# A planned adaLN block on one core: the order of its instructions and loads is made anew

## The chip, the cores and the metric

The kernel runs on one core of a Trainium2 chip. The metric is the device time of one execution in microseconds. Below, PE is TensorE, ACT ScalarE, DVE VectorE, POOL GpSimd and SP SyncE, which here only issues DMAs.

## What is computed

One transformer block with adaptive layer norm, for one sequence of S = 2048 rows and D = 640 columns, all in bfloat16:

```python
mod = (_silu(c) @ w_mod).reshape(c.shape[0], 6, 1, -1)
sa, ca, ga, sb, cb, gb = (mod[:, i] for i in range(6))
h = _layernorm(x) * (1 + ca) + sa
x = x + ga * _A_ref(h, A_wqkv, A_wo)          # 32 heads of 20, causal window of 256
h = _layernorm(x) * (1 + cb) + sb
x = x + gb * _B_ref(h, B_w_gate, B_w_up, B_w_down)   # (sigmoid(h wg) * (h wu)) wd, 1536 wide
```

(The loop over i stands for six assignments.) `w_mod` has 640 rows and 3840 columns; wqkv 640 x 1920, wo 640 x 640, the gate and up weights 640 x 1536, the down weight 1536 x 640.

## The kernel before, in words

**Chunks and blocks.** The sequence is cut into 8 chunks `a` of 256 rows, each of two blocks `b` of 128 rows. Per chunk there are these steps: load the two x blocks (tags x0 to x15, `load_x` with pool `x0`, four buffers); layer-norm statistics and normalization (`ln_stats`: `bn_stats` on L721, `bn_aggr` on L723, the power on POOL, L728, the normalization on L731); a transpose into `hT`, for chunks 0 and 1 by PE (`pe_transposes`), later by DMA (`transp_dma`), with scale and shift (`modulate`, L745 and L746); q, k and v projections (`qkv`, evacuated by `evac` on L792 of ACT or L793 of DVE), transposes of q and k; attention in score sets (four heads each, `score_set`: matmuls on L871, one exponential over 128 x 2048 on L882 of ACT, masks on POOL, L890 and L892), then `burst` with the product with v and its normalization (`norm`, L933 to L942), written to DRAM and read back transposed as `oT`; the output projection plus residual (`outproj`, L987), for which x is loaded a second time (tags y0 to y15, pool `x1`, six buffers); a second layer norm; the gated product (`mlp`, L1025, L1027), the down projection and the second residual add (L1042); the store.

Nearly all matmuls show one line of the helper `mm`, L636 (whole tiles) or L637 (tiles of heads), and all plain DMAs show L524.

**Weights and modulation.** All weights are loaded once and stay. The three thirds of `w_mod` are loaded first into memory that later holds other things: third 0 (`wm0`) into `wd`, third 1 (`wm1`) into `wu`, third 2 (`wm2`) into `hh`. Their products with silu(c) give the shifts and scales for the two layer norms, and `gbc`, by which DVE multiplies `wo` (L1066) and `wd` (L1011). Third 0 is needed before the first `hT` (copy `mA`, L707); `shB` (L1060) is a short DVE copy of another product.

**The order.** Nothing runs in the order in which the program names it. Each step is recorded by `Prog.op` with a list of engines, a planned duration, its dependencies, a priority (`prio` plus an entry of the table `PRI` by tag) and an earliest time `tmin`. `Prog.schedule` then places one step after the other: for each engine it takes, of the steps whose planned start lies within a small width of the earliest (0.04 us, for PE `PE_EPS`), that of the lowest priority number; of the engines it takes the one that starts first. Buffers are handed out in the same pass. For DMAs the plan has one variable `bw`, the time up to which the 16 DMA engines are taken. `emit` writes the order of each engine out as a fixed program with semaphore waits. The plan's times are used for nothing else: on the chip each engine goes through its list, and an instruction waits for its semaphores with all that stands behind it on its engine.

**Queues.** All DMAs go to SP but three: `c_row` and the x blocks 0 and 1, which ACT issues. The large loads (wv, wm1, wo, wm2, wg, wu, wd) are a chain: each waits for the one three places ahead of it (`chain`, DEEP = 3). Score sets have an earliest planned time `PACE0 + PACE * n`.

**Before, at the start,** SP issues x2, five parts of wm0, two of wq, two of wk, x3, wv and on; ACT issues x0, c_row, x1. PE runs matmuls on zeros until the first products with `w_mod` are there.

Of the kernel before, what the change touches and what calls it, by code (L numbers as in the profile page):

```python
# [8 lines left out]
ALU = mybir.AluOpType  # L9
# [5 lines left out]
H = 32  # L15
DH = 20
# [64 lines left out]
class Prog:  # L81
# [67 lines left out]
    def schedule(self):  # L149
        free = {e: 0.0 for e in ENGS}  # L150
        bw = 0.0
# [68 lines left out]
        while placed < n:  # L220
            best = None
            for e in ENGS:
# [5 lines left out]
                for o in c.values():  # L228
                    st = max(free[e] + (SWITCH if e == "pe" and o.mode != pemode else 0.0), o.ready)
                    if e == "dve" and o.port:  # L230
                        st = max(st, free["pool"])
                    elif e == "pool":
                        st = max(st, portend)
                    if o.tiles:
                        got = slots_for(o)
                        if got is None:
                            continue
                        st = max(st, got[0])
                    lst.append((st, o))
                    if tmin is None or st < tmin:  # L240
                        tmin = st
# [26 lines left out]
            if o.isdma:  # L268
                s0 = max(st + dur + 1.1, bw)
                bw = s0 + o.work  # L270
                o.end = bw + 0.7
# [118 lines left out]
def c_pe(n):  # L390
# [3 lines left out]
PE_EPS = 0.131  # L394
PRI = {
    "amodu2": 50.6, "amodu3": 100.7, "amodu4": 71.5, "amodu5": -83.8, "amodu6": 14.5, "amodu7": 25.1, "apow0": 50.2,
    "apow1": -22.7, "apow2": -37.9, "apow3": 26.2, "apow4": 37.9, "apow5": 2.4, "apow6": -29.7, "apow7": 20.3,
    "astats0": 2.8, "astats1": 0.5, "astats2": 0.4, "astats3": 134.9, "astats4": 103.8, "astats5": 149.6,
    "astats6": 33.7, "astats7": -18.8, "atr2": -1.5, "atr3": 36.3, "atr4": 0.4, "atr5": 6.4, "atr6": -17.8,
    "atr7": 32.3, "axh0": -4.4, "axh1": 29, "axh2": -1.6, "axh3": -4, "axh4": 6.9, "axh5": 15.3, "axh6": 0.6,  # L400
    "bmodu0": 11.1, "bmodu1": 54, "bmodu2": -3, "bmodu3": -7.5, "bmodu4": -47.5, "bmodu5": -2.3, "bmodu6": 5.7,
    "bmodu7": 60.8, "bpow0": -33.2, "bpow1": 14.6, "bpow2": 1.5, "bpow3": 1, "bpow4": 39.4, "bpow5": 82.1,
    "bpow6": -42.5, "bpow7": -21.3, "bstats0": 108.1, "bstats1": 8.1, "bstats3": 41.3, "bstats4": 61.6,
    "bstats5": 2.3, "bstats6": -14.7, "bstats7": -15.8, "btr0": 17.3, "btr1": 57.4, "btr2": 19.5, "btr3": 8.1,
    "btr4": 10.3, "btr5": 35.7, "btr6": -1.2, "btr7": -3.5, "bxh0": -14.2, "bxh1": -11.3, "bxh2": 18.2, "bxh3": -5.2,
    "bxh4": 2, "bxh5": 10.7, "bxh6": 59.4, "ctr": -8.6, "divide_0": -2.5, "divide_1": -38.1, "divide_2": -302.1,
    "divide_3": -25.2, "divide_4": 0.3, "divide_5": 32.3, "divide_6": -19.5, "divide_7": 20.5, "down0": 188.3,
    "down1": -19.9, "down2": -6.2, "down3": 118.6, "down4": 39.9, "down5": 1.1, "down6": 189.9, "down7": 296.8,
    "evqk0": -26.7, "evqk1": 40.4, "evqk2": 55.5, "evqk3": 11.1, "evqk4": 136.1, "evqk5": 44.7, "evqk6": -9.9,
    "evqk7": -0.3, "evqt0": -5, "evqt1": 5.6, "evv0": -5.5, "evv1": -10.9, "evv2": -29.4, "evv3": 1.8, "evv4": -1.8,  # L410
    "evv5": -0.4, "evv6": -4.1, "evv7": -12.7, "exp0": -20.6, "exp1": -20, "exp2": 18.1, "exp3": -0.8, "exp4": 35,
    "exp5": 41.7, "exp6": -96.1, "exp7": 17, "fill": -28.3, "glu_0": -19, "glu_1": 32.2, "glu_2": -32.7,
    "glu_3": 3.6, "glu_4": 6.6, "glu_6": -34.6, "glu_7": 63.5, "hTe0": 26.9, "hTe1": -6.9, "mask0": 27.5,
    "mask1": 25.2, "mask2": -21, "mask3": -12.1, "mask4": 63.1, "mask5": 16.4, "mask6": -2.3, "mask7": -22.1,
    "mlpg0": -25, "mlpg1": -24.5, "mlpg2": -24, "mlpu0": -25, "mlpu1": -24.5, "mlpu2": -24, "modA": -31.1,
    "modb": 2.1, "modc": -5.5, "n_ow_1": -73.7, "n_ow_2": -67, "n_ow_3": -11.5, "n_ow_4": 36.5, "n_ow_5": -4.9,
    "n_ow_6": 29.3, "n_ow_7": -1.9, "oT_0": 1.4, "oT_1": 16.1, "oT_2": 4.4, "oT_3": 37.2, "oT_4": 2.4, "oT_6": -15.9,
    "oT_7": -3.4, "out": -15.4, "projk0": -19.5, "projk2": 143.9, "projk3": -25.9, "projk4": 13.2, "projk5": 135.4,
    "projk6": -9.3, "projk7": -118.9, "projq0": -0.3, "projq3": -6, "projq4": 40.3, "projq5": 52.7, "projq6": -169.6,
    "projq7": -38.9, "projv2": 2.9, "projv3": 4.3, "projv4": 41.9, "projv5": 112.6, "projv7": 9.5, "ptr0": 6.6,  # L420
    "ptr1": 1.9, "pv1": -153.5, "pv2": -0.8, "pv3": -128.5, "pv4": 17.1, "pv5": -199.3, "pv6": 1.1, "pv7": 4,
    "qkt2": -0.1, "qkt3": 23.5, "qkt4": 210.5, "qkt6": -3.3, "qkt7": 39.1, "qtr0": -33.3, "qtr1": 1.7,
    "recip_0": -12.7, "recip_1": 25.7, "recip_2": -20.5, "recip_3": 18.8, "recip_4": 9.7, "recip_5": 75.9,
    "recip_7": 12.6, "res1_0": -27.2, "res1_1": -8.7, "res1_2": -8.7, "res1_3": 25.5, "res1_4": -28.5,
    "res1_5": -9.5, "res1_6": 10.7, "res1_7": 67.4, "res2_0": -5.2, "res2_1": -14.6, "res2_2": -0.5, "res2_3": 22,
    "res2_4": -19.6, "res2_5": -24.6, "res2_6": 93.7, "res2_7": 8.4, "score0": -27.9, "score1": -134.6,
    "score2": -18.3, "score3": -59.5, "score4": -289.6, "score5": 2.5, "score6": -20, "score7": -7.8, "tanh_0": 24.5,
    "tanh_1": 2.1, "tanh_2": -28.6, "tanh_3": -25.9, "tanh_4": -6.8, "tanh_5": 6.3, "tanh_6": 11.9, "tanh_7": 38.4,
    "tr1_1": 6.2, "tr1_2": -10.2, "tr1_3": -0.8, "tr1_5": -13.6, "tr1_6": 21.6, "tr1_7": 3.7, "tr2_0": -27.5,
    "tr2_1": 3.6, "tr2_2": 17.6, "tr2_3": 66.8, "tr2_4": 32, "tr2_5": -3.1, "tr2_6": 0.9, "tr2_7": -9.7, "wd": 3.7,  # L430
    "wds": -3, "wg": 8.7, "wk": -26.3, "wm0": -103, "wm1": 71.9, "wm2": -53.2, "wo": -48, "wo0": -23.5, "wo1": 4.4,
    "wo2": 13, "wo3": 15.4, "wo4": 24.1, "wo5": 28.9, "wo6": 29.6, "wo7": 14.8, "wos": 119.8, "wq": -27.7,
    "wu": 43.3, "wv": 3.2, "x0": -72.7, "x1": 14.7, "x10": 86.9, "x11": 65.2, "x12": 113.8, "x13": 107.7,
    "x14": 140.6, "x15": 301.2, "x2": -111.6, "x3": -19.2, "x4": 5, "x5": 8.7, "x6": 45.4, "x7": 45.5, "x8": 52.8,
    "x9": 60.4, "y0": -5.3, "y1": 45.5, "y10": 144.4, "y11": 91, "y12": 118.4, "y13": 163.1, "y14": 327.3,
    "y15": 235.6, "y2": 29, "y3": 73.8, "y4": 85.7, "y5": 17.2, "y6": 87.2, "y7": 163, "y9": 116.1,
# [6 lines left out]
PACE0 = -16.86  # L443
PACE = -0.757
# [4 lines left out]
WSE = ['dve', 'dve']  # L449


def build(nc, A_x, A_wqkv, A_wo, B_x, B_w_gate, B_w_up, B_w_down, c, w_mod, out, S=2048):
# [66 lines left out]
    def dma(dst, src, work, reads=(), writes=(), prio=50.0, tmin=0.0, tag="dma", extra=(), nonc=False, hold=(), eng="sp"):  # L519
# [5 lines left out]
        return A(eng, fn, 0.45, reads=reads, writes=writes, prio=prio, work=work, tmin=tmin, tag=tag, extra=extra, hold=hold)  # L525

    bulk = []

    def chain():
        return [bulk[-DEEP]] if len(bulk) >= DEEP else []  # L530
# [23 lines left out]
    def load_x(pool, b, prio, tmin=0.0, eng="sp"):  # L554
        t = Tile(pool, f"{pool.name}_{b}")
        dma(lambda: t.ap[:], lambda: x_flat[b * 128:(b + 1) * 128, :], 0.47 if b > 1 else 0.9, writes=[t.r()], prio=prio, tmin=tmin, tag=f"x{b}" if pool is p_x0 else f"y{b}",
            eng=eng)
# [9 lines left out]
    def load_wm(i, kt, prio, tmin=0.0):  # L567
        if i:
            bulk.append(dma(lambda: wm_ap[i][:, kt, :], lambda: wm_src[:, kt, i * 1280:(i + 1) * 1280], 0.86,
                            writes=[Rm[i][kt]], prio=prio, tag=f"wm{i}", extra=chain()))  # L570
            return bulk[-1]
        return dma(lambda: wm_ap[i][:, kt, :], lambda: wm_src[:, kt, i * 1280:(i + 1) * 1280], 1.12 - 0.06 * kt, writes=[Rm[i][kt]],
                   prio=prio, tmin=tmin, tag=f"wm{i}")

# [3 lines left out]
    def load_w3(k, prio, halves):  # L578
# [4 lines left out]
        if k == "wv":  # L583
            bulk.append(o)

# [8 lines left out]
    for kt in range(NDT):  # L594
        load_wm(1, kt, 0.4 + 0.01 * kt)
    bulk.append(dma(lambda: wo[:], lambda: A_wo.rearrange("(t p) f -> p t f", p=128), 2.2, writes=[R_wo], prio=0.5, tag="wo",
                    extra=chain()))
    for kt in range(NDT):
        load_wm(2, kt, 0.6 + 0.01 * kt)
# [109 lines left out]
    for kt in range(NDT):  # L709
        bulk.append(dma(lambda kt=kt: wg[:, kt, :], lambda kt=kt: B_w_gate.rearrange("(t p) f -> p t f", p=128)[:, kt, :], 1.03,  # L710
                        writes=[R_wg[kt]], prio=0.7 + 0.01 * kt, tag="wg", extra=chain()))

    def ln_stats(src, dst, prio, ln, a):
# [3 lines left out]
        def v(lo, w):  # L717
            return st.ap[:, lo:lo + w]
# [11 lines left out]
        for bi in range(n):  # L730
            A("dve", lambda e, g, bi=bi: e.tensor_scalar(dst[bi].ap[:], src[bi].ap[:], v(24 + 2 * bi, 1), v(30 + bi, 1),  # L731
                                                         op0=ALU.subtract, op1=ALU.mult), 0.44, port=True,
# [392 lines left out]
```

## Time and profile before

| what | value |
|---|---|
| median of 6 runs | 338.58 us (337.53 to 343.88) |
| the profiled execution, its own time | 338.71 us |
| its span, first to last instruction | 337.0 us |
| mean granted TensorE clock | 1.000 |
| DMA | 38.72 MB, mean 115 GB/s |
| first projection with wq | starts at 12.83 us |
| last matmul ends, last add starts | 334.7 us |

In the lines of the profile each engine has a busy time, its share of the span, and the number of instructions; PEld are the weight loads of TensorE. A row of forty digits cuts the span into equal slices of 8.4 us; a digit is the busy share in tenths. A line of windows has the stretch, its length, then busy time and number of instructions of PE, PEld, DVE, ACT and POOL, the granted clock, the DMA share and GB/s. A line of waits says which engine and line waited, for whom, then microseconds in total, how often, and the longest. A line of the timeline has start, length, engine, source line, operation, output and inputs; in brackets stands the idle time of the engine before it and what ended it.

### The profile page before, as it was taken

The page shows a single profiled execution, that of the slowest core. Times are in us where ns is not written, and L with a number is a line of the kernel's source. Part 1 is how long each engine was busy: PE and PEld are TensorE (multiplying, and loading weights), DVE is VectorE, ACT ScalarE, POOL GpSimd, SP SyncE. Part 2 cuts the span into 40 slices and gives each one's busy share as a digit, 9 for nine tenths or more (in the row PEclk, how much of TensorE's full clock was granted, in tenths as well). Part 3 has the DMA queues.
Part 4 walks back from the last instruction along what each step waited for, and adds up shares of the span by engine and source line. Part 5 has one row for each costly group of instructions (what it writes and reads, how often), then busy time and mean ns, then how long its engine had stood idle before and what let it go on. Part 6 is the DMA issues. An engine that isn't in the chain of part 4 may idle for free.

```text
span 337.0 us, 10072 instructions
## 1 busy us (share of the span) xinstructions
PE 326.2 (97%) x4146; PEld 232.2 (69%) x4146; DVE 227.4 (67%) x469; ACT 226.8 (67%) x215; POOL 160.8 (48%) x232
## 2 busy tenths in 40 slices
PE   8798989999899999999999999999999999999997
PEld 3555645657676667676666766776677787887875
DVE  5497988999889958553868567765558673553232
ACT  1386888897888989787889777897699440121200
POOL 4135466565587755575656674866576500010000
DMA  7987999979942981641383024220234041221001
GB/s 250 377 258 248 263 348 174 198 158 187 228 128 53 132 152 23 77 90 60 94 125 87 4 58 120 60 42 21 73 106 60 18 67 36 62 41 39 2 19 58
DMA packets 71686, 38.72 MB, mean 115 GB/s; under 512 B 46682, under 2 KB 68442, under 8 KB 71642
## 3 DMA queue, kind: packets, MB, share of 16 engines
q1 hardware_dynamic: 71344, 37.76, 48.4%
q8 instruction: 32, 0.52, 0.7%
q10 hardware_dynamic: 298, 0.33, 0.3%
q14 instruction: 12, 0.10, 0.1%
HBM read 21.96 MB, written 5.24 MB: 81 GB/s over the span
## 4 chain that ended last, share of the span: by engine, by line
PE 80%; DMA 10%; DVE 5%; issue 2%; ACT 1%; POOL 1%; SPq 0%; ACTq 0%; DVEq 0%
PE M L636 67%; PE S L637 7%; PE M L637 6%; DMA x<-in_A_x_dram 3%; DMA hT<-x 3%; DMA hh<-in_w_mod_dram 3%; DVE st L721 1%; DVE x L731 1%; DVE h2T L746 1%; DVE stg L793 1%; ACT E L882 1%; POOL st L728 0%; DVE T L933 0%; DVE hT L746 0%; SPq L524 0%
## 5 line engine op out<-in xcount | busy, mean ns | idle before, releaser
L882 ACT ACTIVATE E<-S 128x2048 bf16<-128x2048 f32 x90 | 168.9, 1877 | 30.3 <-PE S L637 28.8
L890 POOL TENSOR_SCALAR_AFFINE_SELECT E<-E 128x512 bf16<-128x512 bf16 (+2 forms) x90 | 77.2, 857 | 88.4 <-ACT E L882 88.1
L892 POOL TENSOR_SCALAR_AFFINE_SELECT E<-E 128x512 bf16<-128x512 bf16 (+1 forms) x84 | 69.4, 826 | 0.0
L636 PE MATMUL M<-h2T,wg 128*128 128x256 bf16 x480 | 63.1, 273 | 0.2 <-DVE h2T L746 0.2
L636 PE MATMUL M<-h2T,wu 128*128 128x256 bf16 x480 | 62.7, 273 | 0.0
L1025 ACT ACTIVATE sig<-M 128x512 f32<-128x512 f32 x48 | 28.6, 595 | 44.8 <-PE M L636 44.7
L1027 DVE SCALAR_TENSOR_TENSOR hh<-sig,M 128x512 bf16<-128x512 f32 x48 | 32.5, 677 | 35.4 <-PE M L636 26.5
L636 PE MATMUL M<-wd,hh 128*128 128x320 bf16 (+2 forms) x396 | 55.4, 295 | 0.0
L636 PEld LDWEIGHTS M<-h2T,wg 128*128 128x128 bf16 x480 | 44.9, 98 | 9.9 <-issue 2.5
L636 PEld LDWEIGHTS M<-h2T,wu 128*128 128x128 bf16 x480 | 45.7, 98 | 7.8 <-issue 2.1
L636 PEld LDWEIGHTS M<-wd,hh 128*128 128x128 bf16 x396 | 37.3, 98 | 14.8 <-issue 1.3
L637 PE MATMUL S<-QT,KT 20*128 20x256 bf16 (+1 forms) x960 | 35.9, 245 | 0.9 <-ACT E L882 0.9
L1042 DVE TENSOR_TENSOR x<-M,x 128x320 bf16<-128x320 f32 (+2 forms) x33 | 15.9, 481 | 26.5 <-PE M L636 26.3
L721 DVE BATCH_NORM_STATS2 st<-x 128x6 f32<-128x320 bf16 x64 | 28.9, 477 | 5.9 <-DMA x<-in_A_x_dram 5.8
L637 PEld LDWEIGHTS S<-QT,KT 20*128 20x128 bf16 x960 | 14.1, 92 | 21.0 <-ACT E L882 17.5
L933 DVE STREAM_TRANSPOSE T<-M 128x512 f32<-128x512 f32 x32 | 21.1, 694 | 10.8 <-PE M L637 10.7
L636 PE MATMUL M<-wq,hT 128*128 128x320 bf16 x160 | 25.3, 300 | 1.8 <-DVE stg L793 1.7
L726 POOL TENSOR_SCALAR st<-st 128x2 f32<-128x2 f32 x16 | 3.8, 235 | 46.2 <-DVE st L723 46.2
L636 PE MATMUL M<-wk,hT 128*128 128x320 bf16 x160 | 25.3, 300 | 0.2 <-DVE hT L746 0.2
L636 PE MATMUL M<-wv,hT 128*128 128x320 bf16 x160 | 25.1, 300 | 0.2 <-issue 0.2
L636 PE MATMUL M<-wo,oT 128*128 128x320 bf16 x160 | 24.6, 300 | 0.0
L637 PE MATMUL M<-E,V 128*32 128x256 bf16 (+1 forms) x960 | 22.7, 246 | 1.3 <-DVE shB L1060 1.2
(73 smaller groups left out, 318.5 us busy)
## 6 DMA issues: line engine op xcount, KB each, us to landing
x<-in_A_x_dram SPq DMA_DIRECT2D x30, 160.0 KB
doc<-On SPq DMA_DIRECT2D x64, 40.0 KB
out_dram<-x SPq DMA_DIRECT2D x15, 160.0 KB
wg<-in_B_w_gate_dram SPq DMA_DIRECT2D x5, 384.0 KB
wu<-in_B_w_up_dram SPq DMA_DIRECT2D x5, 384.0 KB
wd<-in_B_w_down_dram SPq DMA_DIRECT2D x4, 480.0 KB
wd<-in_w_mod_dram SPq DMA_DIRECT2D x5, 320.0 KB
wu<-in_w_mod_dram SPq DMA_DIRECT2D x5, 320.0 KB
```

The lines of the kernel that those rows point to most:

```text
L636: return e.matmul(o, l, r, start=st, stop=sp, skip_group_check=True)
L637: return e.matmul(o, l, r, start=st, stop=sp, tile_position=tp, skip_group_check=True)
L721: A("dve", lambda e, g, bi=bi, j=j: e.bn_stats(v(bi * 12 + j * 6, 6), src[bi].ap[:, j * 320:(j + 1) * 320]), 0.48, reads=[src[bi].r()], wr ...
L726: A("pool", lambda e, g: e.tensor_scalar(v(28, n), var(), EPS, None, op0=ALU.add), 0.2, reads=[st.r(("m", bi)) for bi in range(n)], writes ...
L731: A("dve", lambda e, g, bi=bi: e.tensor_scalar(dst[bi].ap[:], src[bi].ap[:], v(24 + 2 * bi, 1), v(30 + bi, 1), op0=ALU.subtract, op1=ALU.m ...
L882: A("act", lambda e, eng: e.activation(E.ap[:], Sp.ap[:], ACT.Exp, scale=SM_SCALE), 1.876, reads=[Sp.r()], writes=[E.r()], prio=3, tag=f"e ...
L890: return e.affine_select(ap, ap, pattern=[[0, ap.shape[1]], [1, 128]], compare_op=ALU.is_ge, fill=0.0, base=0, channel_multiplier=-1)
L892: return e.affine_select(ap, ap, pattern=[[0, ap.shape[1]], [-1, 128]], compare_op=ALU.is_ge, fill=0.0, base=-1, channel_multiplier=1)
L933: A("dve", lambda e, g, h=h: e.transpose(T1.ap[:, 512 * h:512 * h + 512], X[h].ap), 0.694, reads=[X[h].r()], writes=[T1.r(h)], prio=3.5, t ...
L1025: A("act", lambda e, g, pg=pg, sg=sg: e.activation(sg.ap[:], pg.ap[:], ACT.Tanh, scale=0.5), c_act(512), reads=[pg.r()], writes=[sg.r()], ...
L1027: A("dve", lambda e, g, pu=pu, sg=sg, f0=f0: e.scalar_tensor_tensor(out=hh.ap[:, f0:f0 + 2, :], in0=sg.ap[:].rearrange("p (a b) -> p a b", ...
L1042: A("dve", lambda e, g, ps=ps, bi=bi, c0=c0, n=n: e.tensor_tensor(x1[bi].ap[:, c0:c0 + n], ps.ap[:, 0:n], x1[bi].ap[:, c0:c0 + n], op=ALU. ...
```

## The change

The table `PRI` is replaced as a whole, with PE_EPS, PACE0 and PACE. In the planner DMAs get two variables `bw`, one for SP's and one for ACT's queue, which share the rate while both are taken, and a DMA is not planned to start while its queue has more than QMAX = 4.5 us of planned work ahead. x0 and x1 get a planned latency 1.2 instead of 0.05, and residual loads an earliest planned time of 40 + 30a instead of 40. The code has new switches: several parts of a weight in one load (BN), another queue for the chain (BQ), evacuations and adds of two PSUM banks at once (PAIR, PAIRO), other engines for normalization and modulation (XHE, MOE). They stand at values under which the recorded steps, their sizes and their engines to choose from are those of before. The table is said to have been searched with each order judged by a dozen random draws of the plan.

The diff, cut to its core:

```diff
-        bw = 0.0
+        bw = [0.0, 0.0]
...
+                    if o.isdma:
+                        st = max(st, bw[e != "sp"] - QMAX)
...
-                s0 = max(st + dur + 1.1, bw)
-                bw = s0 + o.work
-                o.end = bw + 0.7
+                k = e != "sp"
+                s0 = max(st + dur + 1.1, bw[k])
+                share = min(o.work, max(0.0, bw[1 - k] - s0))
+                bw[k] = s0 + o.work + share
+                bw[1 - k] += share
+                o.end = bw[k] + 0.7
...
-PE_EPS = 0.131
+PE_EPS = 0.121
 PRI = {
...
-    "wds": -3, "wg": 8.7, "wk": -26.3, "wm0": -103, "wm1": 71.9, "wm2": -53.2, "wo": -48, "wo0": -23.5, "wo1": 4.4,
...
-    "wu": 43.3, "wv": 3.2, "x0": -72.7, "x1": 14.7, "x10": 86.9, "x11": 65.2, "x12": 113.8, "x13": 107.7,
-    "x14": 140.6, "x15": 301.2, "x2": -111.6, "x3": -19.2, "x4": 5, "x5": 8.7, "x6": 45.4, "x7": 45.5, "x8": 52.8,
-    "x9": 60.4, "y0": -5.3, "y1": 45.5, "y10": 144.4, "y11": 91, "y12": 118.4, "y13": 163.1, "y14": 327.3,
-    "y15": 235.6, "y2": 29, "y3": 73.8, "y4": 85.7, "y5": 17.2, "y6": 87.2, "y7": 163, "y9": 116.1,
...
+    "tr2_7": -14.2, "wd": -0.2, "wds": 17.7, "wg": -0.1, "wm1": 73.7, "wm2": 52, "wo": -10, "wo0": 8.2, "wo1": 2,
+    "wo2": 20.9, "wo3": -5.2, "wo4": 15, "wo5": 28.9, "wo6": 2.2, "wo7": -4.4, "wos": -9.4, "wu": 1.9, "x10": 759,
+    "x11": 630.2, "x12": 639.2, "x13": 636.1, "x14": 1004.5, "x15": 1060.3, "x4": 520.7, "x5": 428.9, "x6": 397.3,
+    "x7": 0.1, "x8": 564.9, "x9": 604.2, "y0": 4.2, "y1": 32.8, "y10": 17.9, "y11": 31.3, "y12": -29.1, "y13": -2.4,
+    "y14": -9.3, "y15": 5.5, "y2": 27.8, "y3": 51.5, "y4": 20.2, "y5": 22.5, "y6": 93.1, "y7": -24.3, "y8": 74.8,
+    "y9": 18.4,
 }
...
-PACE0 = -16.86
-PACE = -0.757
+PACE0 = 27.19
+PACE = 0.664
...
-WSE = ['dve', 'dve']
+WSE = ("dve", "dve")
+BQ = "sp"
+BN = 5
+QMAX = 4.5
+PAIR = 0
+PAIRO = 0
+XHE = ("dve",)
+MOE = ("dve", "act")
...
-        return [bulk[-DEEP]] if len(bulk) >= DEEP else []
+        return [bulk[-DEEP]] if len(bulk) >= DEEP else front
...
-            eng=eng)
+            eng=eng, lat=0.05 if b > 1 else 1.2)
...
+    def load_bulk(dst, src, Rs, work, prio, tag, extra=()):
+
+        n = len(Rs)
+        k = 0
+        while k < n:
+            m = min(k + -(-n // BN), n)
+            bulk.append(dma(lambda k=k, m=m: dst[:, k:m, :], lambda k=k, m=m: src[:, k:m, :], work * (m - k), writes=Rs[k:m],
+                            prio=prio + 0.01 * k, tag=tag, extra=list(extra) + chain(), eng=BQ,
+                            dur=0.37 + 0.08 * (m - k)))
+            k = m
...
-        x1 = [load_x(p_x1, 2 * a + bi, 15, tmin=40.0) for bi in range(2)]
+        x1 = [load_x(p_x1, 2 * a + bi, 15, tmin=40.0 + 30.0 * a) for bi in range(2)]
```

The base priorities to which the table is added stand in the calls: x0 and x1 0, wm0 0.20 to 0.24, wq 0.30, wk 0.31, x2 0.32, x3 0.33, wv 0.34, wm1 from 0.4, wo 0.5, x4 to x7 0.55, wm2 from 0.6, wg from 0.7, wu from 0.8, wd from 0.9, x8 and later 20 + 0.1a, residual loads 15.

## The prediction

> **What bounds the kernel now.** I read the engine shares first, then the forty slices, then TensorE's stretches, then its waits, and last what lies behind the two longest waits.
>
> From the page, the shares and the slices:
>
> ```profile
> PE 326.2 (97%) x4146; PEld 232.2 (69%) x4146; DVE 227.4 (67%) x469; ACT 226.8 (67%) x215; POOL 160.8 (48%) x232
> ...
> PE   8798989999899999999999999999999999999997
> ...
> DMA  7987999979942981641383024220234041221001
> ```
>
> TensorE (PE) is the bound over nearly the whole span, and its digits below 9 lie in the first eleven slices and the last. DMA is full over the first nine to eleven slices too, then it is slack. So what can still be won is where loads compete.
>
> The windows of TensorE from the first projection to the last matmul (busy, number of matmuls):
>
> ```profile
> 12.80:92.50 79.70, 74.34 (x975) 49.19 (x973) 68.53 (x154) 65.68 (x73) 41.06 (x53) 1.00 0.97 238
> 92.50:268.43 175.93, 175.69 (x2527) 123.78 (x2524) 122.35 (x236) 146.87 (x119) 114.20 (x150) 1.00 0.38 76
> 268.43:334.71 66.28, 66.26 (x566) 54.56 (x566) 29.63 (x59) 12.12 (x21) 0.93 (x2) 1.00 0.16 39
> ```
>
> From 92.5 us on, TensorE idles 0.24 + 0.02 us of 242 us: nothing is to be won there, only lost. Between 12.8 and 92.5 it idles 79.70 - 74.34 = 5.36 us, with DMA at a share of 0.97. Ahead of 12.8 is the head, behind 334.71 a tail of 2.3 us (last residual add, store).
>
> TensorE's waits in 12.8 to 92.5:
>
> ```profile
> PE M L636 <- DVE stg L793: 1.7, 1, 1.7
> PE M L637 <- DVE shB L1060: 1.2, 1, 1.2
> PE S L637 <- ACT E L882: 0.9, 1, 0.9
> PE M L636 <- DVE hT L767: 0.8, 3, 0.4
> PE M L636 <- DMA hh<-in_w_mod_dram: 0.4, 1, 0.4
> ```
>
> Three waits make 3.8 of the 5.4 us. The timeline of VectorE (DVE) shows what stood ahead of the instruction that TensorE waited for:
>
> ```profile
> 28.99 0.49 DVE L721 BATCH_NORM_STATS2 st<-x 128x6 f32<-128x320 bf16 x1 [1.42 <-DMA x<-in_A_x_dram]
> 29.40 0.15 DVE L1060 COPY shB<-M 128x5 f32<-128x5 f32 x1
> ...
> 48.10 0.89 DVE L721 BATCH_NORM_STATS2 st<-x 128x6 f32<-128x320 bf16 x2 [0.59 <-DMA x<-in_A_x_dram]
> 49.90 0.49 DVE L721 BATCH_NORM_STATS2 st<-x 128x6 f32<-128x320 bf16 x1 [0.91 <-DMA x<-in_A_x_dram]
> 50.31 0.47 DVE L793 CAST stg<-M 128x320 bf16<-128x320 f32 x1
> ```
>
> Both times layer-norm statistics waited for an x block, and a short evacuation stood behind them on VectorE. The third wait (92.17 us) is ScalarE's: its exponential stood behind a modulation (L745) that waited 0.89 us for a transpose DMA, 7.2 us long in the chain of waits (81.97 to 89.17). So one cause covers all three: a load that lands late in a full DMA phase, and an in-order queue that passes the delay on.
>
> **What the Trainium skill says.** "Perfetto Trace Analysis", Per-engine timelines: ScalarE, VectorE and GpSimd run strictly in order. The trace agrees: the 0.15 us copy at 29.40 started only when the late statistics had begun, and TensorE lost 1.25 us. "DMA: Bandwidth & Descriptors", Issuing engines are not separate DMA queues: loads issued from SP and ScalarE share the same 16 engines. The trace agrees: x of block 1, alone on ScalarE's queue with 160 KB, took 6.0 us to land. The same page, under Queues, rings and completion order, says that the engines take turns between queues packet by packet. By that, x1 should not have to wait for all of w_mod; the trace speaks against it (243 GB/s over the first 7.84 us are 1.9 MB, nearly all of x0, x1, x2 and the five w_mod parts, 2.08 MB together). I go by the measurement: x1 lands about with the last byte issued ahead of it.
>
> **The change part by part.** First what costs nothing. The new switches stand at BN = 5, BQ = SP and PAIR = PAIRO = 0; load_bulk so makes five loads of one part each, as before; evacuations and adds keep their halves; XHE and MOE name the engines of before. No instruction is added or taken away, no DMA changes size, and the chain of bulk loads waits as before (front stays empty). QMAX, lat and the second bw exist only in the planner. What changes is the order on five in-order queues, and with it which semaphore is late. So matmul time is kept: 316.29 us busy from 12.80 to 334.71.
>
> *Head.* Priorities: x2 (-111.3 summed) stood first on SP, ahead of w_mod (-102.8). Now x2 has 0.32, behind five w_mod, two wq and two wk loads. 160 KB leave the front; the 5 us window of 5 to 10 us moved 327 GB/s, so x1 and w_mod may land 160/327 = 0.49 us earlier. Against that: on ScalarE's queue x0 went first (0.78), then c_row, then x1 (1.84). Now c_row (-1) is first, x0 second, so x0 is issued some 0.5 us later (c_row's issue took 0.58) and behind a w_mod part; x1 keeps its place. x0's statistics are covered: x0 was in at 3.72, x1 at 7.84, and in between lie x0's statistics and, with x2 early, x2's (four of 0.44 and two of 0.2 us, to 6.2). If x0 lands with x1, its own 1.1 us come on the path; x2's 1.1 us move into the stretch of 15 to 25 us, where VectorE is busy 9.3 of 10 us and chunk 1's evacuations already hold TensorE 0.8 us. Bounds of the head -0.5 and +1.7; I take -0.2. From x1 to the first projection are 7.84 to 12.83 = 5.0 us of statistics, GpSimd power (0.95), normalization, transposes, evacuation; that stays.
>
> *Residual loads.* Six x1 buffers let y0 to y5 go at 40 us; ten x loads are issued between 42 and 60. By summed priorities y0 (9.7), y5 (32), y2 (44) and y1 (60.5) went before x8 (73) and x9 (81), the blocks that VectorE waits for at 48 to 50. The new tmin, 40 + 30a, leaves y0 and y1 there and puts y2, y3 past 70 and y4, y5 past 100 us of plan time. At least two loads go from ahead of x8 and x9: 320 KB at 378 GB/s (window 48 to 50) = 0.85 us; with y4 as well as later ones up to 640 KB = 1.7 us. VectorE's waits were 0.59 + 0.91 = 1.50 us. I take most of TensorE's 1.71 us as gone: -1.4 (bounds 0 and -1.7). What is late next is the hT transpose of chunk 3 issued at 47.68, no worse than before. Later y loads fall where the DMA share is 0.38, so they should be in time; VectorE's 3.8 us wait for a residual (L987) came after 200 us and cost TensorE nothing that the list of waits shows.
>
> *x of later chunks.* Their priorities go from 5 to 300 to about 400 to 1060 (x7 alone 0.1), so on SP they yield to everything ready. This clears the weights' and transposes' way, but delays x itself. For the wait at 28.45 (1.25 us) I take half, -0.6, bounds -1.25 and +1.7 (one further stall of the size seen at 49 us). For the wait at 91.3 (0.86 us): wd and x loads were issued among the transposes at 77 to 82 us; without two of them 0.85 us less stands ahead. I take -0.4, bounds -0.86 and +0.9.
>
> *Pace and tie width.* Score sets may start from 27.19 + 0.664n; exponentials come every 2.4 us or so, so after the first sets the pace never binds. PE_EPS 0.121 instead of 0.131 only reorders ties. Zero, but for the saturated stretch after 92.5 us any new order can only lose: +0.2, bounds 0 and +2.
>
> *Sum:* -0.2 - 1.4 - 0.6 - 0.4 + 0.2 = -2.4 us. The profiled execution took 338.71 (span 337.0 and 1.7 around it), 0.13 above the median of 338.58. 338.6 - 2.4 = 336.2 us.
>
> **The rivals.**
> - *x comes too late (slower).* Place: chunks 2 to 5, 25 to 95 us. An x block yields on SP to weights, its statistics block VectorE, TensorE waits for an evacuation behind them. Price: 1.7 us a time, as at 49 us. For it: x4 to x11 now stand behind every other load, and DMA is full until 63 us. Against: the plan puts the statistics later as well if it knows the delay. It decides from the point where VectorE's wait for x in 12.8 to 92.5 us passes some 5 us (2.9 now). With the present gaps kept, two more stalls and the head's 0.2 gained: 338.6 + 3.4 - 0.2 = 341.8 us.
> - *The gaps only move.* TensorE stalls 5 us elsewhere because planned and real landing times differ as much as before. For it: the present order has its gaps just there. Against: the named residual loads really leave. 338.6 us.
> - *Everything goes.* All 5.36 us of idle and the head's 0.5 go, with 0.2 lost later: 338.6 - 5.7 = 332.9 us. Against: three waits of the 5.36 (chunk 1's evacuations, 0.8) hang on no load.
> - That the change doesn't do what it says can't be excluded for the head: with c_row first, x0 isn't first on its queue. It is priced above.
>
> **How the numbers follow.** Forecast (334.5 to 337.6) 0.60, gaps only move 0.15, too late 0.16, everything goes 0.09. The likeliest gives 336.2. An eighty per cent range keeps the forecast, the unmoved case, the better part of everything goes and the start of too late: 332.9 to 340.2. A measurement of this kernel tells some 0.3%, 1.0 us, from no change. Faster than 337.6: 0.58 + 0.08 = 0.66; within: 0.13 of gaps moved and 0.04 from the edges, 0.17; slower: 0.17.
>
> **What would show it.** Right: from the first projection to the end of the crowded phase TensorE idles about 3 us instead of 5.36; no wait of a projection for stg behind statistics near 49 us; residual loads spread over the span; busy TensorE time unchanged; x1 in by about 7.4 us. Wrong: VectorE waiting for x longer than 2.9 us in that stretch, a first projection later than 12.8 us, or TensorE idle of more than 0.5 us past 92.5 us, where each microsecond adds fully to the time.

## The result, and the profile after

The changed kernel takes 341.75 us (median of 17 runs, 339.13 to 343.77), the kernel before in the same measurement 338.66 us (38 runs). The ratio is 1.0084, 95% interval 1.0058 to 1.011. Measured again later, it was 1.0064 (1.0039 to 1.009). The forecast of 336.2 us had the wrong sign, and its range (to 340.2) didn't reach the result.

The profiled execution took 342.81 us. Its shares and slices, with one row that the page of before doesn't have, PEclk, the clock granted to TensorE in tenths:

```profile
PE 328.8 (96%) x4146; PEld 234.2 (69%) x4146; DVE 229.6 (67%) x461; ACT 231.3 (68%) x223; POOL 160.6 (47%) x232
...
PE   8997799988999999999999999999999999999997
...
PEclk9996999999999999999999999999999999999999
DMA  7987998699980295012786016410321121211001
```

In the fourth slice TensorE ran at a lowered clock: by windows of 1 us it was 0.50 from 29 to 35 us, about 3.1 us of matmul time lost. So this one execution mixes two things. A second profile of the same kernel (run e11_after_again below; 339.90 us, span 338.2) had the full clock throughout. The windows of that execution, from the first wq projection to the last matmul:

```profile
11.84:94.00 82.16, 75.89 (x985) 50.11 (x987) 69.03 (x148) 69.41 (x80) 44.38 (x56) 1.00 0.94 233
94.00:277.00 183.00, 182.08 (x2584) 129.91 (x2577) 129.18 (x250) 149.53 (x125) 111.06 (x147) 1.00 0.36 75
277.00:335.89 58.89, 58.89 (x500) 47.95 (x497) 24.00 (x47) 9.84 (x18) 0.93 (x2) 1.00 0.13 38
```

With the profile of before cut in the same way (12.83 to 94, to 277, to 334.70: 316.26 us busy, idle 5.36 + 0.24 + 0.01), the two balance out. The head is 0.99 us shorter; TensorE idles 6.27 instead of 5.36 us up to 94 us, 0.92 instead of 0.24 us later; matmul time is 316.87, 0.61 us more. -0.99 + 0.91 + 0.67 + 0.61 = +1.2 us, and the last matmul ends at 335.89 instead of 334.70. (This execution is a quick one: fourteen of this kernel at full clock had a mean of 340.53.) TensorE's waits up to 94 us in it:

```profile
PE M L658 <- DMA oT<-doc: 1.4, 1, 1.4
PE M L659 <- DVE stg L813: 1.3, 1, 1.3
PE M L658 <- DMA hh<-in_w_mod_dram: 1.1, 1, 1.1
PE M L658 <- DVE KT L813: 1.1, 1, 1.1
PE M L658 <- DVE h2T L766: 0.4, 1, 0.4
```

The three long waits of before (the projection's stg at 50 us, shB, the exponential E at 92 us) are gone. Four others of the same size stand in their place. One of them is new in kind. The timeline of VectorE and GpSimd ahead of the wait for stg, in the same execution (GpSimd's mask is AFFINE_SELECT):

```profile
74.54 2.48 DVE L751 TENSOR_SCALAR x<-x,st 128x640 bf16<-128x640 bf16 x2
74.63 1.09 POOL L932 TENSOR_SCALAR_AFFINE_SELECT E<-E 128x1024 bf16<-128x1024 bf16 x1 [0.78 <-ACT E L924]
...
75.67 1.17 POOL L934 TENSOR_SCALAR_AFFINE_SELECT E<-E 128x1024 bf16<-128x1024 bf16 x1
...
76.95 0.87 DVE L741 BATCH_NORM_STATS2 st<-x 128x6 f32<-128x320 bf16 x2
...
77.74 0.47 DVE L813 CAST stg<-M 128x320 bf16<-128x320 f32 x1
...
78.83 1.39 PE L659 MATMUL M<-E,V 128*32 128x256 bf16 x56 [1.25 <-DVE stg L813]
```

A pair of normalizations (L751) takes 2.48 us here and 0.80 us where no mask runs; the evacuation that TensorE needs stands behind it. The Trainium skill says why this can be: "SBUF — State Buffer", Who interferes with whom, has VectorE and GpSimd share one pair of ports under an exclusive lock: one of them holds it for a whole instruction, and the other is fully blocked. On VectorE's side it applies to instructions that use both ports, and tensor_scalar, which the normalization is, can be one. The trace agrees: the pair ends, at 77.02, 0.18 us after the second mask (76.84). In the same execution 14 of the 32 normalizations took more than 0.5 us, and each of them ended 0.18 us after a mask; one alone takes some 0.44 us. The group of all 32 before and after (busy time of the group, then mean ns of one):

```profile
L731 DVE TENSOR_SCALAR x<-x,st 128x640 bf16<-128x640 bf16 x32 | 18.4, 601 | 6.3 <-POOL st L728 6.2
L751 DVE TENSOR_SCALAR x<-x,st 128x640 bf16<-128x640 bf16 x32 | 21.8, 720 | 3.4 <-POOL st L748 3.4
```

The second line is e11's; the first profile of the changed kernel has 24.2 us and 794 ns.

The planner knows of this lock. `schedule` doesn't place a VectorE step marked `port` before GpSimd is free, nor a GpSimd step before such a step has ended (`portend`, L230 to L233 of the changed code, the same in the code before). But `emit` writes no semaphore for it: on the chip it holds only while the timing keeps to the plan.

### The profile page after: what moved, and what is told of

It is laid out like the page before. It is cut to its first block, busy times and chain, and to the rows that moved or that the text cites. A ratio compares the mean times of both kernels' runs of the same rounds, so it can differ in the third digit from the quotient of the medians.

```text
span 341.0 us, 10076 instructions
## 1 busy us (share of the span) xinstructions
PE 328.8 (96%) x4146; PEld 234.2 (69%) x4146; DVE 229.6 (67%) x461; ACT 231.3 (68%) x223; POOL 160.6 (47%) x232
## 4 chain that ended last, share of the span: by engine, by line
PE 86%; DVE 6%; DMA 5%; issue 1%; SPq 1%; POOL 0%; ACTq 0%; DVEq 0%
PE M L658 72%; PE S L659 8%; PE M L659 6%; DMA hh<-in_w_mod_dram 2%; DVE x L751 2%; DMA x<-in_A_x_dram 2%; DVE st L741 1%; DMA oT<-doc 1%; DVE h2T L766 1%; DVE wd L1064 1%; SPq L757 0%; SPq L536 0%; DVE T L975 0%; DVE gbc L706 0%; ACTq L536 0%
## 5 line engine op out<-in xcount | busy, mean ns | idle before, releaser
L934 POOL TENSOR_SCALAR_AFFINE_SELECT E<-E 128x512 bf16<-128x512 bf16 (+1 forms) x84 | 68.3, 813 | 0.0
L658 PE MATMUL M<-h2T,wu 128*128 128x256 bf16 x480 | 64.4, 273 | 0.5 <-DVE hh L1080 0.5
L658 PE MATMUL M<-h2T,wg 128*128 128x256 bf16 x480 | 61.3, 273 | 0.4 <-DVE h2T L766 0.4
L658 PEld LDWEIGHTS M<-h2T,wu 128*128 128x128 bf16 x480 | 44.8, 98 | 10.3 <-issue 3.8
L658 PEld LDWEIGHTS M<-h2T,wg 128*128 128x128 bf16 x480 | 45.8, 98 | 8.2 <-DVE h2T L766 1.4
L741 DVE BATCH_NORM_STATS2 st<-x 128x6 f32<-128x320 bf16 x64 | 28.2, 476 | 3.4 <-DMA x<-in_A_x_dram 3.2
L658 PE MATMUL M<-wq,hT 128*128 128x320 bf16 x160 | 26.8, 308 | 0.0
L751 DVE TENSOR_SCALAR x<-x,st 128x640 bf16<-128x640 bf16 x32 | 24.2, 794 | 3.5 <-POOL st L748 3.5
```

What stands on the lines that cost most here:

```text
L658: return e.matmul(o, l, r, start=st, stop=sp, skip_group_check=True)
L741: A("dve", lambda e, g, bi=bi, j=j: e.bn_stats(v(bi * 12 + j * 6, 6), src[bi].ap[:, j * 320:(j + 1) * 320]), 0.48, reads=[src[bi].r()], wr ...
L751: A(XHE, lambda e, g, bi=bi: e.tensor_scalar(dst[bi].ap[:], src[bi].ap[:], v(24 + 2 * bi, 1), v(30 + bi, 1), op0=ALU.subtract, op1=ALU.mul ...
L934: return e.affine_select(ap, ap, pattern=[[0, ap.shape[1]], [-1, 128]], compare_op=ALU.is_ge, fill=0.0, base=-1, channel_multiplier=1)
```

## The experiments

Except for e11, which is the changed kernel itself, each kernel puts a function `reorder(P)` between `P.schedule()` and `P.emit()`, which edits the finished plan; `nth`, `put_before` and `put_after` find and move steps in an engine's list. The last column gives the mean of the executions at full clock and their number; the kernel before had 338.65, 338.39, 338.47 and 338.18 there, in the groups e1 to e4, e5 to e8, e9 to e11, and e12.

| kernel | median us | ratio to before (95%) | full clock: mean, number |
|---|---|---|---|
| e1_fill | 340.39 | 1.0013 (0.9991 to 1.0035) | 340.35, 21 of 22 |
| e2_wm2_first | 343.65 | 1.0103 (1.0065 to 1.014) | 342.61, 1 of 8 |
| e3_port | 338.67 | 0.9975 (0.9953 to 0.9997) | 338.51, 19 of 22 |
| e4_before_head | 338.40 | 0.9973 (0.9951 to 0.9996) | 338.08, 7 of 22 |
| e5_before_port | 339.30 | 1.0002 (0.9969 to 1.0035) | 337.61, 5 of 14 |
| e6_head_port | 338.47 | 0.9976 (0.9951 to 1.0001) | 337.89, 9 of 22 |
| e7_port_fill | 338.04 | 0.9968 (0.9945 to 0.9991) | 338.27, 22 of 22 |
| e8_res_late | 340.07 | 1.0017 (0.9994 to 1.0039) | 339.49, 13 of 22 |
| e9_port_two | 340.84 | 1.0048 (1.0024 to 1.0072) | 340.05, 14 of 22 |
| e10_port_rest | 340.44 | 1.0042 (1.0022 to 1.0062) | 339.49, 8 of 22 |
| e11_after_again | 341.18 | 1.0064 (1.0039 to 1.009) | 340.53, 14 of 22 |
| e12_port_modu_fill | 337.31 | 0.9933 (0.991 to 0.9956) | 337.29, 21 of 22 |

**e1_fill: is it the lowered clock?** In the first profile a wait of 2.2 us for the last third of `w_mod` came right before the drop. The edit gives TensorE work there (a query projection issued eight times, into the same result):

```diff
+    o = pe[pe.index(nth(pe, "modc", 5)) - 1]
+    o.fn = lambda e, g, fn=o.fn: [fn(e, g) for _ in range(8)][-1]
```

> The changed kernel; the two matmuls of a q projection that stand just ahead of the first product with the last third of w_mod on TensorE are done eight times instead of once (the same values into the same place), which fills some 2.0 us of the 2.2 us that TensorE waits there. Theory A (the wait itself is long enough for the granted clock to fall to half for 3.4 to 7 us afterwards): granted clock 1.00 in the profile and in every execution, no slice below 9 in the clock row, and 340.0 to 340.8 us, about 1 to 1.5 us better than 341.75, since about half of the executions showed a lowered clock. Theory B (loads of x come too late and block VectorE) and theory C (the stretch up to 63 us is limited by loads, TensorE only waits elsewhere): time stays at 341.5 to 342 us, whatever the clock row shows.

The drop is gone: 21 of 22 executions ran at full clock, against 24 of 40 for the changed kernel in both measurements. So the drop of the changed kernel follows from this gap, and one costs about 2 us (340.81 at full clock, 342.53 below, in the first measurement). But at full clock 340.35 us is still 1.7 above before. And before had a lowered clock as often, in 96 of 214 executions. The clock isn't the difference between the two kernels.

**e2_wm2_first: is it the late third of w_mod?** Its first two loads go ahead of x5 on SP.

```diff
+    put_before(sp, [nth(sp, "wm2", 0), nth(sp, "wm2", 1)], nth(sp, "x5", 0))
```

> The changed kernel; on SP's queue the first two parts of the last third of w_mod are issued ahead of x5, wo and x4. Theory A: the first part lands 2 to 3 us earlier, TensorE's wait of 2.2 us falls under 0.5 us, the clock stays at 1.00, and the time is 338 to 339.5 us. Theory B: x5 and x4 come some 1.8 us later (640 KB at 350 GB/s), the statistics of chunk 2 block VectorE longer, and the time is 342.5 to 344 us. Theory C: the wait at 27 us goes and another of like size comes by 45 us (for wo, x4 or the later parts); only the clock's share is won, 340 to 341 us.

It made things worse. The wait for `hh` went, but the statistics of x4 now waited 4.68 us, and TensorE 4.58 us for an evacuation behind them. So the late place of these loads isn't what cost the time. This is also what the rival "x comes too late" looks like when it does occur.

**e3_port: is it the shared port?** The GpSimd step planned next after a normalization (tag `axh` or `bxh`) gets that normalization as a dependency, so that one direction of the plan's lock holds on the chip. A normalization still doesn't wait for a mask that is placed ahead of it.

```diff
+    for d in P.order["dve"]:
+        if "xh" in d.tag:
+            later = [p for p in P.order["pool"] if p.start >= d.start]
+            if later:
+                later[0].deps.append(d)
```

> The changed kernel; after each normalization on VectorE the mask on GpSimd that the plan places next waits for it with a semaphore, so the two no longer run at once. Theory D (the normalizations take 794 instead of 601 ns on average because masks on GpSimd hold VectorE up, and TensorE's waits near 41 and 81 us, 1.5 and 1.25 us, come from that): the mean falls to 450 to 600 ns, the two waits fall to under 0.5 us each, and the time is 339.5 to 340.5 us. Theory A alone: both waits may go but the time falls by at most 0.5 us. Theory C: the waits move to the loads behind them, 341 to 342 us.

338.67 us: the whole loss is gone, with one kind of wait added and nothing taken away. The normalizations and TensorE's windows in the profile of this run:

```profile
L777 DVE TENSOR_SCALAR x<-x,st 128x640 bf16<-128x640 bf16 x32 | 14.8, 502 | 3.5 <-POOL st L774 3.5
12.03:94.00 81.97, 76.89 (x995) 50.61 (x994) 66.27 (x151) 70.52 (x82) 43.20 (x56) 1.00 0.98 234
94.00:277.00 183.00, 182.46 (x2585) 130.74 (x2583) 126.93 (x248) 149.68 (x124) 111.38 (x147) 1.00 0.37 75
```

Up to 94 us TensorE idles 5.08 us where e11 has 6.27, and behind it 0.54 instead of 0.92: 1.57 us less in all. Four normalizations still take more than 0.5 us, beside masks that the rule doesn't cover. The same place as above, in the profile of this run:

```profile
74.54 0.49 DVE L839 CAST stg<-M 128x320 bf16<-128x320 f32 x1 [0.19 <-PE M L684]
74.95 0.80 DVE L777 TENSOR_SCALAR x<-x,st 128x640 bf16<-128x640 bf16 x2
75.88 1.09 POOL L958 TENSOR_SCALAR_AFFINE_SELECT E<-E 128x1024 bf16<-128x1024 bf16 x1 [1.61 <-DVE x L777]
76.46 0.47 DVE L839 CAST stg<-M 128x320 bf16<-128x320 f32 x1
```

The pair takes 0.80 us, the mask waits for it, and the evacuation no longer stands behind 2.5 us. TensorE's long waits for oT (1.5), `hh` (1.0) and KT (1.0) are still there, so they aren't what the rule took away.

**e4_before_head: the head alone.** The kernel before, with the start of the changed one:

```diff
+    put_after(sp, [nth(sp, "x2", 0)], nth(sp, "wk", 1))
+    put_after(act, [nth(act, "x0", 0)], act[1])
...
+    put_before(dve, [dve[7], dve[10], dve[12]], dve[4])
+    put_before(dve, st[:3], st[3])
+    put_after(pe, [nth(pe, "ctr", 0)], nth(pe, "warm", 1))
+    put_before(pe, [nth(pe, "modA", 5)], nth(pe, "ptr0", 0))
```

> The kernel before, with the changed kernel's head only: x2 behind the two wk loads on SP, c_row ahead of x0 on ScalarE, silu(c) ahead of x0's statistics and x2's statistics behind the first evacuations on VectorE, the small product with c and the last product with the first third of w_mod earlier on TensorE. All theories: first projection with wq at 11.3 to 11.8 us instead of 12.83. If the head adds up with the rest: 337.0 to 337.6 us. Theory C: TensorE's idle time from the first projection to 92 us grows by 1 to 1.5 us beyond 5.36, and the time is 338.2 to 339 us. Theory A: if a single wait grows past about 2 us, the clock falls after it and the time is 340 us or more.

0.9973 is 0.9 us of gain over all executions; at full clock it is 0.6 us (338.08 to 338.65), from seven executions. The first projection starts at 11.30 instead of 12.83 us. The head of the change is good.

**e5_before_port: does the rule help before too?** The rule of e3 on the kernel before.

> The kernel before with the rule of e3_port: each planned GpSimd instruction that follows a normalization waits for that normalization. The port theory says that the collisions are what the change made worse: the normalization's 32 instructions took 18.4 us in the kernel before, 24.2 us in the kernel after and 14.8 us under the rule, so before has 3.6 us of surplus where after has 9.4. After gained 2.3 us by the rule (at full clock), so before should gain in proportion 0.9 us, at most 1.2 (ratio to before 0.9965 to 0.9985), with a mean normalization near 500 ns. The rival, that the rule helps any order alike and the collisions do not tell the two kernels apart, expects 2 us or more (ratio 0.994 or lower). If the collisions cost before nothing, because its surplus lies where TensorE does not wait, the ratio is 1.000 within its interval.

A normalization takes 485 ns on average (four of 32 still above 0.5 us, twelve without the rule), so most collisions are gone here as well, but the time is the same: 1.0002, with an interval that excludes the 2 us that the changed kernel gained. The five executions at full clock (337.61) leave room for some 0.8 us. The timelines fit this: in the profile of before, the first normalization above 0.5 us comes at 54.2 us, and TensorE's only wait above 0.3 us from there to the last matmul is the one for the exponential at 91 us, which the prediction traces to a transpose. So before has collisions too, but none on which TensorE waits for long. What is particular to the changed kernel is that some of its collisions lie where TensorE waits for what is queued behind them.

**e6_head_port** has head and rule on the kernel before together.

> The kernel before with the head of after (as in e4_before_head) and the rule of e3_port. If the head's gain (0.9 us, measured in e4_before_head) and the rule's (0.9 us expected) are independent, the ratio to before is 0.994 to 0.9955, 337.0 us. If an earlier start only makes TensorE wait longer for the same thing later, the two do not add: 0.9965 to 0.998.

0.9976, the same as with the head alone. The rule adds nothing, as in e5.

**e7_port_fill** is the changed kernel with e3 and e1 together.

> The kernel after with both the rule of e3_port and the filling of e1_fill (one query projection ahead of a modulation product issued eight times, which changes no result). The rule gave 0.9975 with 3 of 22 executions at a lowered clock, so what filling can add is small: 0.1 to 0.4 us, less its own cost if TensorE does not wait there: ratio to before 0.9965 to 0.998. If the wait for the modulation weights at 27 to 29 us is the larger part of what after loses, filling gives more than 0.8 us in addition (ratio 0.995 or lower).

0.9968, as expected: all 22 executions ran at full clock, but e3 alone already had 19 of 22 there.

**e8_res_late: the residual loads.** The forecast's largest term, by itself, on the kernel before:

```diff
+    put_after(sp, [nth(sp, t, 0) for t in ("y0", "y8", "y5", "y2")], nth(sp, "x10", 0))
```

> The kernel before with four residual loads (y0, y8, y5, y2, 640 KB in all) moved on SP from right behind x9 to behind x10, some 10 us later; nothing else. The forecast's step on the residual loads expects that the wait of 1.7 us at 49 us goes, most of it: -1.4 us, ratio 0.996. The order theory says that x8 and x9, for which VectorE waits there, stand ahead of these loads on SP already, so that the move can at most free some engine time behind them: 0 to -0.4 us, ratio 0.9988 to 1.000, with the wait of the projection for its staging evacuation still there in the profile (1 us or more).

Nothing is gained (1.0017; at full clock it even takes 1.1 us more, 339.49 to 338.39), and the wait is still there: 1.6 us for stg. The two statistics at 48 and 50 us, in VectorE's timeline, wait for x as they did before:

```profile
48.12 0.89 DVE L744 BATCH_NORM_STATS2 st<-x 128x6 f32<-128x320 bf16 x2 [0.63 <-DMA x<-in_A_x_dram]
49.82 0.49 DVE L744 BATCH_NORM_STATS2 st<-x 128x6 f32<-128x320 bf16 x1 [0.81 <-DMA x<-in_A_x_dram]
```

0.63 + 0.81 us here, 0.59 + 0.91 before. On SP, x8 and x9 stand ahead of these four loads in the order of the kernel before (places 40 and 43, y0 44, y8 45, y5 46, y2 47).

**e9_port_two, e10_port_rest, e11_after_again: where do the collisions cost?** e9 has the rule for the pairs at 37 and 77 us only, e10 for all the others, e11 is the changed kernel once more.

```diff
-        if "xh" in d.tag:
+        if d.tag in ("axh3", "bxh0"):
```

> The kernel after with the rule of e3_port for two of the sixteen pairs of normalizations only: those at 37.4 us (2.60 us) and 77.3 us (2.49 us), behind which TensorE waited 1.5 and 1.3 us. The port theory, in its narrow form: these two carry the loss, so that their TensorE waits go and the time falls by 1.5 to 2.5 us, to the ratio of e3_port (0.9975) or up to 1.000. If all sixteen pairs have their share, these two give 0.3 to 0.8 us: ratio 1.004 to 1.007. If order and not the port is the cause, the time stays at that of after in the same call.

> The kernel after with the rule for the other fourteen pairs, not for those at 37.4 and 77.3 us: the complement of e9_port_two. The narrow port theory expects at most 0.7 us of gain on after of this call, since the stretch behind 94 us loses only 0.9 us of TensorE's time in all; if all sixteen have their share, 1.3 to 2.0 us. If both halves gain 2 us each, the rule acts by something else than the pairs it guards.

> The kernel after, unchanged, on the same chip as e9_port_two and e10_port_rest, as their base. The ratio to before of the first measurement, 1.0084 with an interval of 1.0058 to 1.011, should come again; at full clock 2 us above before, with the two long normalizations at 37 and 77 us in a profiled execution at full clock as well, if the lowered clock of the first profile has nothing to do with them.

e11 repeats the loss (1.0064; at full clock 340.53, 2.06 above before). Against it e9 gains 0.5 us and e10 1.0 us at full clock, each within about 0.8 us. Their sum of 1.5 is less than the 2.0 of the whole rule, but not by more than this. My narrow form of the theory, that two pairs carry the loss, falls. One of the two, the pair at 37 us, took 2.60 us in the first profile, where the clock was lowered just before it, but only 0.80 in e11. In e10, at full clock and with this pair unguarded, it collides again:

```profile
34.78 2.02 POOL L958 TENSOR_SCALAR_AFFINE_SELECT E<-E 128x2048 bf16<-128x2048 bf16 x1 [0.19 <-ACT E L950]
34.86 2.47 DVE L777 TENSOR_SCALAR x<-x,st 128x640 bf16<-128x640 bf16 x2
...
37.25 0.48 DVE L1149 TENSOR_TENSOR wo<-wo,gbc 128x640 bf16<-128x640 bf16 x1
37.77 1.02 DVE L732 TENSOR_SCALAR gbc<-M 128x320 bf16<-128x320 f32 x2
38.93 0.84 PE L685 MATMUL M<-E,V 128*32 128x256 bf16 x32 [1.89 <-DVE gbc L732]
```

The mask started 0.08 us ahead of the pair, and TensorE lost 1.89 us. In e11 the mask at this place started 0.13 us behind the second normalization, and that one took its usual 0.44 us. Whether a pair is hit is a matter of a tenth or two of a microsecond, so no fixed place carries the loss.

**e12_port_modu_fill: the better version.** The rule is extended to the modulations, which the code marks `port` too, with the filling of e1:

```diff
-        if "xh" in d.tag:
+        if "xh" in d.tag or "modu" in d.tag:
```

> The kernel after with the rule and the filling of e7_port_fill, and the rule for VectorE's modulations as well (28 of h2T at 445 ns and 17 of hT at 472 ns in e7_port_fill, against 403 ns for h2T in the kernel before). If what the port still costs lies on TensorE's path, the modulations' surplus (28 x 0.04 + 17 x 0.07 = 2.3 us at most) gives back 0.3 to 1 us: ratio to before 0.994 to 0.996. If the masks, which wait longer now, are what the attention products need next, the time rises above e7_port_fill (0.998 or more). The first is the better version, if it holds.

337.31 us, ratio 0.9933 (0.991 to 0.9956): it beats before, and by the ratios of 1.0064 and 1.0084 the changed kernel too. The modulations of `h2T` and TensorE's windows in its profile:

```profile
L795 DVE TENSOR_SCALAR h2T<-h2T,scB,shB 128x256 bf16<-128x256 bf16 x28 | 7.7, 331 | 0.0
```

```profile
12.21:94.00 81.79, 77.99 (x1005) 51.77 (x1004) 64.58 (x153) 70.06 (x81) 42.17 (x55) 1.00 0.95 233
94.00:277.00 183.00, 182.91 (x2591) 131.40 (x2589) 122.64 (x246) 150.08 (x125) 111.99 (x148) 1.00 0.37 75
```

A modulation of `h2T` takes 331 ns (474 in e11, 403 before), and behind 94 us TensorE idles 0.09 us where e11 has 0.92 and e3, without the modulations, 0.54: the loss in that stretch was the port's as well. Against before at full clock the gain is 0.9 us (337.29 to 338.18), where e7, without the modulations, had 0.1 (338.27 to 338.39). The rest of the ratio goes with the clock, which fell in 17 of 27 executions of before in that group and in one of 22 here.

## Why the prediction was wrong

**What costs nothing** failed, and with it the sign. It reasoned that no instruction is added, so only waits can change. For matmuls this held within 0.6 us of 316. For VectorE it didn't: the 32 normalizations took 18.4 us before, 24.2 and 21.8 us in the two profiles after, 14.8 under the rule, which leaves four of them long. The surplus over 14.8 went from 3.6 to 7.0 us at full clock. The page of before showed the sign: a mean of 601 ns for an operation of which a pair takes 0.80 us undisturbed. I never asked what made the mean. The rule shows the worth of this: -2.0 us at full clock (340.53 to 338.51, from two groups of runs; 2.2 us with each taken against before of its own group), the size of the whole loss (2.06). So the step that failed is the one that gave VectorE's work the same length in any order: the prediction put it at nothing, and it cost about 2 us.

**Residual loads, -1.4.** The premise was false. I inferred from summed priorities that y0, y5, y2 and y1 go ahead of x8 and x9. In the finished order of before x8 and x9 stood ahead, since readiness comes before priority in `schedule`, and moving four of the loads gained nothing (e8). The stall at 50 us did vanish in the changed kernel, but not through this step. The order of statistics and evacuations on VectorE is another there, and on SP x8 and x9 stand at places 35 and 37 instead of 40 and 43; no run isolates what removed it.

**What is late next** was where the sum was too hopeful, even without collisions. The forecast took 2.4 us of waits as gone and named little in their place. The changed kernel has waits for oT, `hh` and KT of 1.4, 1.1 and 1.1 us, together 3.6, where before had 3.8 in the three that went. They remain in e3. That was the rival "The gaps only move", and its time (338.6) is nearly that of e3 (338.67), where most collisions are gone. The collisions came on top.

**x of later chunks, -0.6 and -0.4.** The two waits went, as forecast, and others came. The rival "x comes too late" has the right time (341.8) by luck, for a wrong reason: VectorE waited for x 1.4 us in e11 and 3.2 in the first profile, head included, short of the 5 us from which it was to decide.

**Head, -0.2.** Right in sign, too small: 0.99 us by the profile of e11 and 1.48 by the first; in time e4 has 0.9, and 0.6 at full clock. All lie beyond the bound of -0.5, the last of them by less than its noise. x1 landed at 7.05 us in the first profile and at 7.54 in e11, instead of 7.84 (bound 7.4). The reading behind this term, that x1 lands with the last byte issued ahead of it, is too simple: in the trace of before three quarters of its 160 KB were moved by 5.5 us, in turns with SP's loads, and only the rest came later. The move of x2's statistics into the stretch of 15 to 25 us cost TensorE no wait above 0.3 us in e11; in e4's profile it waits 1.5 us for VectorE between 19 and 23.

**The stretch after 92.5 us, +0.2** (bounds 0 and +2): 0.7 us of idle time came (behind 94 us), which e12 takes away again. I named the tests for being wrong rightly, among them "TensorE idle of more than 0.5 us past 92.5 us".

What stays open: which of the moves of the change brought masks and normalizations together. e9 and e10 show that it isn't one pair, and no run here takes single moves of the order back in that stretch. The 0.5 us between the halves and the whole is within what these runs can resolve. The rule also moves masks to a later time; that its gain comes from the normalizations that it frees, and not from this, is read from the timelines (the wait for stg at 78 us) and isn't separated by a run of its own.

## What to carry to other kernels

Where a planner keeps two instructions apart only by its clock, the separation is gone as soon as the chip is off the plan; if the overlap costs more than the wait, write it as a dependency. Look in the profile for operations whose mean lies well above their shortest, and ask what ran beside them, before calling a reordering free of cost. And take the order of a queue from the order that was emitted, not from the priorities that went into it.

## What the runs showed of the hardware that was not expected

Which of the two, mask or normalization, is held up shows in their starts. In the fourteen profiles of this case 132 of 448 normalizations took more than 0.5 us, and every one of them ended 0.18 us after a mask. Where a mask started up to 0.09 us behind a normalization, the normalization was the one held up in 30 of 32 cases. Where the mask started 0.12 to 0.42 us behind it, none of 40 was: there the normalization took 0.35 to 0.5 us. So a normalization can have the earlier start in the profile, by up to 0.09 us, and still be the one that waits.

TensorE's clock can fall without any long wait. The Trainium skill, "TensorE: Matmul & The Clock Gate", Why this matters for your kernels, advises against idle gaps of more than about 3 us. In the profile of e4 no wait of TensorE between 15 and 23 us was longer than 0.5 us, yet the clock fell to half:

```profile
19.00:23.00 4.00, 2.30 (x28) 1.25 (x28) 4.00 (x9) 3.23 (x5) 1.74 (x3) 0.99 0.81 254
23.00:24.00 1.00, 1.00 (x18) 0.37 (x17) 1.00 (x3) 0.31 (x1) 0.53 (x1) 0.50 0.95 335
```

Ahead of the drop TensorE was busy 2.30 of 4 us, most of it with transposes (matmuls with the identity). The other three drops that the profiles show while matmuls ran came during or within 2 us after waits of 2.1 (e6), 2.2 (the first profile of the changed kernel) and 4.6 us (e2), while waits of 1.9 us (e10) passed at full clock. The half clock lasted 3.4 us in e2, e4 and e6 and 6.8 us in the first profile of the changed kernel. Nearly half the executions of the kernel before (96 of 214) had a lowered clock, at about 2 us each; where in the kernel it fell in these isn't recorded. In the changed kernel, repeated matmuls in the gap cost nothing that the full-clock times show (340.35 to 340.53) and took the lowered executions from 16 of 40 to one of 22 (e1).
